# Token weights in blocks of rows, transposed whole, in a new order of steps: a fused attention and MLP kernel on one core

## Chip, cores and metric

One core of one Trainium2 chip. The metric is the device time of one execution in microseconds; lower is better. The core has TensorE (PE; its weight loads are PEld), VectorE (DVE), ScalarE (ACT), GpSimd (POOL) and the queue of SyncE (SP), from which all DMAs of this kernel are issued.

## What is computed

Attention over 8 batches of 8 heads, 576 positions, 64 per head; its output, 8 x 576 x 512, is the input x of the second part. Batch and head are b and h, positions s and t.

```
q_d, k_d, v_d = means of q, k, v over groups of 4 positions          # 144 positions
out_up    = repeat(softmax(q_d k_d^T / 8) v_d, 4)                    # coarse attention
out_local = softmax(q k^T / 8 where |s - t| < 4) v                   # band of 7 positions
x         = out_up + out_local, heads side by side                   # 8 x 576 x 512

theta = x @ w_theta
zr, zi = x * cos(theta), x * sin(theta)
y     = w_tok_r @ zr + w_tok_i @ zi                                  # mixes the 576 positions
u     = x + y
out   = u + max(u @ w_ch, 0)
```

Inputs and output are float32; the kernel computes in bfloat16 with float32 sums.

## The kernel before

**A list of steps.** The work is cut into 1191 small steps, each a word of two letters and an argument, and ORDER (lines 57 to 97) is the one list in which all of them are issued. The two letters name a function in STEPS (line 711), which is called for its next tile in a fixed sequence; the argument is either the engine of a copy (v VectorE, a ScalarE, g GpSimd), one or two banks of PSUM, or a staging slot in base 36. After each step `pin` (line 735) ties every instruction to the one before it on its own engine, so that each engine, and the DMA queue of SP, runs its steps strictly in the order of the list. What orders the engines against one another is data alone: a tile, a bank or a slot that must be ready or free.

**Attention.** For each batch four q and four k loads of two heads each (lq, lk, line 287) go to one of 16 staging slots; cq and ck (line 296) cast them to bfloat16, tp (line 303) transposes nine 128x128 pieces into a pair of banks, ev (line 316) copies the pair out as qT or kT. kd and qd are the means over four positions, on GpSimd in two passes (lines 330, 333, 336) or on VectorE in one (line 322). sd, ed, nd, xn, xd and xc are the coarse attention (scores, exponential, product, division, transpose, copy). The local attention goes in three units of windows a batch: ps (scores, line 482), ex (exponential, line 490), mk (mask, line 501), po (product with v, line 511), nm (division, lines 519 and 520), xt (transpose, line 533), and xa (line 541) adds the coarse part into xT. v comes in ten half windows a batch (lv and lw, line 348; cv casts), save for batch 0, whose v comes in four loads (l1, c1, t1, e1, x1; line 372 casts).

**The second part.** th (line 552) is theta for 128 positions, cs (lines 557 and 558) its cosine and sine, xm (line 591) transposes x, zz (line 616) multiplies both into z; tt, ct, zt and zp or dz are the same for the last 64 positions. mx (line 632) is one mixing product: nine accumulated matmuls of z with the transposed token weights WT (128 x 9 x 576) for 128 features and 288 positions (batch 0 takes its four products for positions 0 to 287 first, the others both halves of a feature group in turn); ua (line 637) adds x. ch (line 662) is u @ w_ch, rl (line 667) the maximum and sum, st (line 671) the store. The last 64 positions of two batches share ht, rt, ss and sr (lines 691, 695, 700). For batches 4 to 7 u is transposed by DMA (du, line 641), for 6 and 7 x as well (dx, line 601), and q and k of batch 7 (dk, line 307).

**The token weights.** lb (line 249) loads nine blocks of 128 rows: 0 to 3 of w_tok_r, 5 to 8 of w_tok_i, and 4 the last 64 rows of both. cb (line 259) casts each into uT, which is free until the first batch is mixed. wp (line 267) makes one row group j of WT: five transposes for 128 source positions, one from each block of w_tok_r (even j) or w_tok_i (odd j); the ninth, for the last 64 positions, takes ten transposes of half width. wc (line 277) copies a row group out, 128 x 576. The sequence of row groups is WPJ (line 42). A row group thus needs five cast blocks.

**Warm matmuls.** wm (line 755) issues matmuls on zeros, whose result nothing reads: the argument's second digit counts those of 512 columns, the third gives one of 64 times so many. Six more are issued with the constants (line 226). An argument of two banks is taken by

```
    def pair(w):
        a, b = sorted(int(x) for x in w)
        return PS[:, a:b + 1:b - a, :]
```

and in ORDER before all two-bank arguments are 01, 23, 45 or 67.

Of the kernel before, what the change touches and what calls it, by code (L numbers as in the profile page):

```python
# [14 lines left out]
P = 128  # L15
B = 8
H = 8
S = 576
# [21 lines left out]
HALF = 64  # L40

WPJ = (0, 2, 4, 6, 1, 3, 5, 7, 8)
# [25 lines left out]
lv9 tp23 nm ts cs cqa th4 lq7 xm5 xt01 th6 evv cs tp23 xa zz cqa tt4 ua tp01 kdg cs ct cqg evv ztv th5 lw evv lw xm7
zz cs tp23 mx6 xm4 kdg zp5 qdg ua eva zz cvv ps01 cqa ps23 lv8 xm7 kdg zz zcv lk4 te ex lw mx6 mx4 ua mx5 sd01 mkv lvb
lw ua ex po67 mkv cva ps23 qdg lca lcc utg ed lce nm mx4 cvg ex lcd lvf ua lk1 po01 lk2 sd67 lw po23 ckg nm cqa nm mx5  # L70
ckg ed tp01 cvg ua lq5 eva tp67 mx4 lq0 cca ua up5 evv cvg ua ccg ccg pv23 mkg ucv vda lk3 qdv ps01 ps67 ex up4 mx5
ccv nd23 ex ua nd01 uca kdg ch5 po67 xn ps23 ckg cka lv9 mx4 xn tp01 lw ex mkg rl nm lk6 cva ckg xd5 sd23 ua cqg xcv
xt67 lv7 eva mx4 lw lv4 lw cvg xa lv8 lw ed xt01 po23 po67 th5 ua ch4 cqa ts cs xa nm nm th0 po23 lqb xt67 rl up1 cs
nm kdg th5 xm0 xa cs xm4 tp23 xm6 tt7 mkg cvg zz th0 lqc ucv zz st up1 cvg up5 ch4 eva ucv ckg ct ucv ch1 zz po23 cs
sd67 lve lva rl mkv te ed cvg pv45 lqd lk1 ztg cqg ch0 rl rl lk2 ch1 qdg nm lq3 vda tp67 nd45 rl cqa xm0 lqf eva lw zz
xn nd23 zp1 utg lw xn tp67 zca lk5 lq9 kdg mx0 up1 ua po45 lv0 eva ckg lk7 ps23 nm lw po67 nm ckg lv4 uca mx0 tp45 lk6
qdg mx1 ua xd0 ps67 ua lv8 ex eva xca ckg sd23 xt45 xa lw mx1 mkg st cvg ua ed mx0 ex mx1 mkv ua th0 po23 ua xt45 ts
cs xa xt67 mx1 xm0 xa th4 xm5 lqb zz ua tt0 kdg xm1 cvv ckg cvv th6 ch7 cqg cka cqg cs ct nm cs lvc cqg lk1 ztv tp23
eva lw th0 rl zz cs cqg zz tp67 evv cvg xm4 zz st zp5 zca ch1 rl cva tp23 mx0 po67 ua eva ps45 lw nm po23 lv2 te ex
lv5 mx1 pv67 lke cqg st mx0 po45 dt vda nm lk7 mkv st lqd po23 ckg ua ua qdg sd67 ch1 qdg nm nm ht0 cka ed rt lv3 up6  # L80
up7 cvg ucv uca nd45 kdg cqg nd23 mx0 xn lw xn ps67 ss ps45 ex ex xd2 mx3 tp67 xcv up2 cva ua uca tp45 lq6 rl evv up0
cqg lw eva ch1 ua lvf xt67 ps23 ucv sd45 xa cva st ex lw lq9 rl lk4 mx0 sd23 ed xt67 ua ckg xa lva qdg lw mkv kdv xt45
mx1 cvg th0 ua st lvb mx6 ua lw ed mkg tp23 ts cs utg lw mx7 cqg xa ua up6 po01 po45 cvg eva uca pv23 tt7 nm vda lq0
nm th6 xm0 zz nd45 ct cs ch1 lv1 xn cva st tp23 nd67 cva xn up0 th4 xm5 th6 zz sr eva xm7 xm5 ps23 lv8 lvc rl uca cs
po01 ch4 zz lw cs nm zz ztg ch7 te ex dz xd6 ch5 cvg rl lw lqe utg rl mkg po01 ps23 st mx4 lw lkd up7 cqg cka st ex
up2 uca nm ch3 rl xt01 kdg st st cvg xcv cva qdg ckg ua xa mkg uca po45 pv67 mx2 nm mx0 ua lk6 sd45 vda lk2 rl lq7
xt67 cqg ua ps23 xa mx1 lv5 ed po45 ua lq3 nm st mkv cqg dt ex dk9 sd23 xt67 ckg ed mx0 mkg du xa nd45 ch1 ckg ua po23
xn po67 th0 ts cs th4 tt5 nm cs nd23 rl dkf nm ct cqg evg dka xm1 xm0 mx6 zz th1 th7 cs dk1 cs xm4 xm5 zz ztv xn ua zz
mx6 zz mx4 po23 ua dz xt01 po67 xd5 ua xcv eva lw evg mx4 nm st mx5 eva du xa mx2 ht3 qdg ua mx4 xt01 ua kdg nm ua utg
ps67 du rt cvv du st ps23 kdg ua te ex ex mx5 mx4 ps67 lvb lv0 lw lw qdv xa lv8 sd23 cva xt01 ua mkv xa mkg mx5 ex st  # L90
lv4 ua po67 ua ed nm sd01 ed po23 mkg cvg ch4 ch5 mx0 nm tt1 lw lw cvg cvg rl sr po67 rl dxd po23 ua nm po45 nm ts ct
nm th0 pv67 th1 dx vda ch2 ztg nd45 st st nd67 du xn du xn cs cs du th3 cs th0 xd1 xt45 xt67 rl xcv cs xt23 xa utg dxc
ch1 dx zz ch0 ch4 xa ss ch5 dz th6 zz ch7 dt du xa tt2 zz th3 dxe dx zz st cs rl th1 mx6 cs mx3 ct st ua rl ztv rl cs
dx7 dx mx2 th6 ht4 rt zz mx1 ua mx0 cs rl mx3 mx6 zz dz rl zz ua ua zz mx7 mx1 mx2 ua ua mx0 ua mx3 ua mx6 ua ua mx1
st ua du mx0 st mx2 ua ss utv ch3 ua ua ua st ua utv ch2 ch1 ch0 ch7 ch6 du ch4 du du du du st rl sr rl du du rl dt
ch1 st st rl st rl st st rl rl ht0 rl st st rm su rt sr ss st
# [4 lines left out]
def kernel(  # L101
# [11 lines left out]
    nc = tc.nc  # L113
# [19 lines left out]
    def bank16(w):  # L133
        return PS[:, int(w), :].bitcast(BF16)
# [20 lines left out]
    rl = tiles(2, [P, 2, 4], "rl", FP32)  # L155
# [6 lines left out]
    cs = tiles(NCS, [P, 2, DM], "cs")  # L162
# [96 lines left out]
    def cb(i, w):  # L259
        to = uT[0][:, i, :] if i < 5 else uT[1][:, i - 5, :]  # L260
        COPY[w](out=to, in_=at.pop(("wtok", i)))

    at = {}

    def wp(j, w):
        ps = at["wp", j] = bank16(w)
        for ri in ((j % 2,) if j < 8 else (0, 1)):
            lo, n = (0, P) if j < 8 else (HALF * ri, HALF)  # L270
            for ct in ((0, 1, 2, 3, 4), (4, 0, 1, 2, 3))[ri]:
                base = P * ct - (HALF if ct == 4 and ri else 0)
                nc.tensor.transpose(out=ps[lo:lo + n, base:base + P],
                                    in_=(uT[ri][:, ct, :] if ct < 4 else uT[0][:, 4, :])[:, P * (j // 2):P * (j // 2) + n],
                                    identity=ident)

    def wc(j, w):
        COPY[w](out=WT[:, j, :], in_=at.pop(("wp", j))[:, 0:S])
# [520 lines left out]
```

## Time and profile before

| | us |
|---|---|
| median of 3 runs | 238.1 (236.89 to 238.81) |
| span of the profiled execution, first to last instruction | 232.1 |
| the runs' median less that span | 6.0 |
| TensorE, VectorE, ScalarE, GpSimd busy in it | 220.7, 191.8, 156.1, 135.5 |
| first mixing product (L632) starts | 37.26 |
| last matmul ends | 227.1 |

The profiled execution's own time around its span is not listed apart. Lines of the profile read: line of the kernel, engine, operation, output <- input, shapes and count; behind them busy microseconds and the mean nanoseconds of one, then how long the engine idled just before and what ended it. In a timeline the two leading numbers are the start and the length in microseconds of the instructions merged in the line. Matmuls follow one another faster than their listed length, which includes their way through the array. A wait names who waited, for what, the total, how often and the longest.

### The profile page before, as it was taken

To read this page: it belongs to the slowest core of one execution; us is meant where nothing else is said; L and a number is where in the kernel's file an instruction comes from. 1 tells how busy PE (TensorE), PEld (TensorE's weight loads), DVE (VectorE), ACT (ScalarE), POOL (GpSimd) and SP (SyncE) were. 2 spreads that over 40 slices of the span, in tenths; PEclk is the share of its full clock that TensorE was granted. 3 is DMA by queue.
4 is the path that set the end of the run, shared out by engine and by line. 5 is a ranking of instruction groups with operands and counts; after the bars stand their busy time and mean duration, and the time that the engine had idled before them with its cause. 6 is when DMAs were issued, how large, how long until landed. Compare 5 with 4: busy or idle time off the path is not lost.

```text
span 232.1 us, 9462 instructions
## 1 busy us (share of the span) xinstructions
PE 220.7 (95%) x3986; PEld 153.2 (66%) x3986; DVE 191.8 (83%) x365; ACT 156.1 (67%) x241; POOL 135.5 (58%) x179
## 2 busy tenths in 40 slices
PE   7998899999998999999999999999999998999991
PEld 2665678777776765776768766676676563767750
DVE  6699999989997988868997997799889967567572
ACT  3359999799877989867976979857766591620000
POOL 7468989869999656897472837767386510000000
PEclk9999999999999999999999999999999999999998
DMA  6999989999999899989606895899957766556676
GB/s 204 382 392 390 298 134 252 365 263 193 264 263 195 224 290 208 203 209 210 174 3 178 226 234 147 293 249 173 153 122 189 144 138 100 154 126 182 138 235 217
DMA packets 76795, 49.41 MB, mean 213 GB/s; under 512 B 61136, under 2 KB 61392, under 8 KB 76752
## 3 DMA queue, kind: packets, MB, share of 16 engines
q1 hardware_dynamic: 76752, 48.81, 84.6%
q8 instruction: 31, 0.51, 1.1%
q14 instruction: 12, 0.10, 0.2%
HBM read 33.98 MB, written 9.44 MB: 187 GB/s over the span
## 4 chain that ended last, share of the span: by engine, by line
PE 72%; DVE 12%; DMA 5%; SPq 3%; issue 3%; ACT 2%; DVEq 0%
PE PS L632 24%; PE PS L662 10%; PE PS L552 9%; PE PS L303 5%; PE PS L755 4%; PE PS L511 3%; DVE xT L541 3%; DMA out_dram<-osb 2%; DVE pm L501 2%; PE PS L591 2%; PE PS L482 2%; DMA st<-xT 2%; SPq L641 2%; PE PS L533 2%; DVE uT L637 2%
## 5 line engine op out<-in xcount | busy, mean ns | idle before, releaser
L632 PE MATMUL PS<-WT,z 128*128 128x288 bf16 x576 | 77.9, 286 | 1.7 <-issue 1.7
L632 PEld LDWEIGHTS <-z 128*128 128x128 bf16 x576 | 53.8, 98 | 17.5 <-issue 2.8
L637 DVE TENSOR_TENSOR uT<-PS,xT 128x288 bf16<-128x288 f32 x64 | 28.1, 450 | 11.4 <-PE PS L632 11.1
L552 PE MATMUL PS<-wth,xT 128*128 128x512 bf16 x128 | 32.3, 380 | 0.7 <-DVE xT L541 0.7
L557 ACT ACTIVATE cs<-PS,pihc 128x512 bf16<-128x512 f32 x32 | 22.3, 696 | 15.1 <-PE PS L552 9.9
L662 PE MATMUL PS<-wch,uT 128*128 128x512 bf16 (+1 forms) x132 | 30.6, 373 | 0.0
L520 DVE TENSOR_TENSOR tmp<-PS,rl 128x512 bf16<-128x512 f32 x40 | 27.7, 692 | 1.4
L541 DVE TENSOR_TENSOR xT<-PS,xdT 128x928 bf16<-128x928 f32 (+1 forms) x24 | 22.7, 952 | 3.4 <-PE PS L533 3.1
L490 ACT ACTIVATE pm<-PS 128x1024 bf16<-128x1024 f32 (+1 forms) x24 | 20.4, 877 | 7.0 <-PE PS L482 2.7
L501 POOL TENSOR_TENSOR pm<-pm,band 128x1024 bf16<-128x1024 bf16 (+1 forms) x13 | 22.2, 1709 | 2.9 <-ACT pm L490 2.9
L667 DVE SCALAR_TENSOR_TENSOR osb<-PS,ur 128x512 f32<-128x512 f32 (+1 forms) x33 | 21.8, 669 | 2.4 <-PE PS L662 1.6
L330 POOL TENSOR_TENSOR two<-kT 128x580 f32<-128x580 bf16 x15 | 17.5, 1163 | 6.1 <-ACT kT L316 5.2
L296 POOL CAST q_tm<-st 128x576 bf16<-128x576 f32 x22 | 14.4, 664 | 10.8 <-DMA st<-in_q_dram 10.8
L662 PEld LDWEIGHTS <-uT 128*128 128x128 bf16 x132 | 12.2, 98 | 12.2 <-issue 0.3
L558 ACT ACTIVATE cs<-PS 128x512 bf16<-128x512 f32 x32 | 19.4, 605 | 0.0
L330 POOL TENSOR_TENSOR two<-qT 128x576 f32<-128x576 bf16 x11 | 12.8, 1167 | 10.5 <-ACT qT L316 7.1
L552 PEld LDWEIGHTS <-xT 128*128 128x128 bf16 x128 | 11.2, 98 | 10.7 <-issue 1.3
L616 DVE TENSOR_TENSOR z<-PS,cs 128x1024 bf16<-128x1024 bf16 x24 | 16.2, 685 | 1.9 <-PE PS L591 0.9
L437 ACT ACTIVATE pd<-PS 128x864 bf16<-128x864 f32 x16 | 14.1, 889 | 5.2 <-PE PS L426 5.2
L761 ACT ACT_TABLE_LOAD x13 | 16.7, 1283 | 0.2
L296 POOL CAST k_tm<-st 128x576 bf16<-128x576 f32 x21 | 14.4, 695 | 1.4 <-DMA st<-in_k_dram 1.4
L396 POOL CAST v_w<-st 128x512 bf16<-128x512 f32 x21 | 13.3, 653 | 1.3 <-DMA st<-in_v_dram 1.2
(119 smaller groups left out, 419.3 us busy)
## 6 DMA issues: line engine op xcount, KB each, us to landing
st<-in_q_dram SPq DMA_DIRECT2D x32, 288.0 KB, 6.3
st<-in_k_dram SPq DMA_DIRECT2D x32, 288.0 KB, 6.0
st<-in_v_dram SPq DMA_DIRECT2D x70, 128.0 KB, 4.7
out_dram<-osb SPq DMA_DIRECT2D x31, 256.0 KB, 2.9
out_dram<-osb SPq DMA_DIRECT2D x10, 128.0 KB, 2.4
st<-in_v_dram SPq DMA_DIRECT2D x4, 288.0 KB, 3.7
st<-in_moe_w_tok_r_dram SPq DMA_DIRECT2D x4, 288.0 KB, 6.2
st<-in_moe_w_tok_i_dram SPq DMA_DIRECT2D x4, 288.0 KB, 7.2
```

What stands on the lines that cost most here:

```text
L296: COPY[w](out=to[:, r, :], in_=of[:, r, :])
L330: nc.gpsimd.tensor_tensor(out=t, in0=src[:, :, 0:2], in1=src[:, :, 2:4], op=ALU.add)
L490: nc.scalar.activation(out=pm[(3 * b + u) % NPM][:, :, 0:n].rearrange("p e c j w -> p e (c j w)"), in_=at.pop(("ps", b, u))[:, :, 0:4 * W ...
L501: EW[w].tensor_tensor(out=t, in0=t, in1=m, op=ALU.mult)
L520: nc.vector.tensor_tensor(out=tmp[(NCH * b + c) % NTMP].rearrange("p g (j d) -> p g j d", d=D), in0=ps[:, :, :, 0:D], in1=r.unsqueeze(3).t ...
L541: nc.vector.tensor_tensor(out=xT[b % 2][:, :, lo:lo + cnt].rearrange("p e (m j) -> p e m j", j=4), in0=at.pop(("xt", b, u))[:, :, 0:cnt].r ...
L552: nc.tensor.matmul(out=ps, lhsT=xT[b % 2][:, dc, P * c:P * c + P], rhs=wth[:, dc, :], start=(dc == 0), stop=(dc == 3))
L557: nc.scalar.activation(out=t[:, 0, :], in_=ps, func=AF.Sin, bias=pihc, scale=1.0)
L632: nc.tensor.matmul(out=ps, lhsT=z[b % 2][:, j, P * dc:P * dc + P], rhs=WT[:, j, cols], start=(j == 0), stop=(j == 8))
L637: nc.vector.tensor_tensor(out=uT[b % 2][:, dc, cols], in0=at.pop(("mx", b, i)), in1=xT[b % 2][:, dc, cols], op=ALU.add)
L662: nc.tensor.matmul(out=ps[:, cols], lhsT=uT[b % 2][:, dc, P * c:P * c + P], rhs=wch[:, dc, cols], start=(dc == 0), stop=(dc == 3))
L667: nc.vector.scalar_tensor_tensor(out=o[:, cols], in0=at["ch", b, c][:, cols], scalar=0.0, in1=ur[b % 2][:, c, cols], op0=ALU.max, op1=ALU.add)
```

## The change

Three things. First, the sequence of the token-weight blocks, for loads, casts, transposes and copies alike: WTI = (0, 5, 1, 6, 2, 7, 3, 8, 4), real and imaginary rows in turn, in place of 0 to 8 for loads and casts and WPJ for the rest. Second, wp and wc work on one block of rows instead of one row group of WT: block i is transposed in five whole 128x128 pieces, the fifth from its last 128 columns (448 to 575), of which the lower 64 output partitions alone are used; wc copies four pieces at once into the 128 columns of every second row group, and a tail of 64 partitions into row group 8. Block 4 holds the last 64 rows of both weights: its four pieces fill columns 512 to 575 of all eight row groups, and it has two tails of 64 columns.

Third, ORDER is a new list of 1190 words. All steps are there as before; the places, engines, banks and slots are others, and two-bank arguments may be any two neighbours (34, 56 and 12 among them; pv, which takes two single banks, has 47 once and 36 once). Besides the places these counts change: warm matmuls, 40 of 512 columns and 31 times 64 columns before, 24 and 24 after; q and k casts on ScalarE, GpSimd and VectorE, 20, 43 and 1 before, 13, 32 and 19 after; q/k evictions (ev) 21, 2 and 9 before, 24, 2 and 6 after; query means (qd) 11 on GpSimd and 5 on VectorE before, 16 on GpSimd after; masks (mk) 13 on GpSimd and 11 on VectorE before, 16 and 8 after; v casts 11, 21 and 8 on ScalarE, GpSimd and VectorE before, 17, 17 and 6 after.

```diff
-WPJ = (0, 2, 4, 6, 1, 3, 5, 7, 8)
+WTI = (0, 5, 1, 6, 2, 7, 3, 8, 4)
...
-l10 l11 l12 c1v c1a c1g k0 l13 kcv wm061 t101 c1g lq4 e1v wm256 t123 lk5 lk6 kca e1v wm483 x12 x13 lk7 ckv lq8 x10 cka
...
-zz zz lw qdv lk8 wcv eva ct lk4 lq9 cs cbg cbg cbg cbg wp6 wca wp3 wp2 wp4 wp5 wca wp1 wcv wcv wcv wp2 ztg ps67 ps45
-qdg wcv te ex wcv ex lq7 kdg lkb lka zz lkc lqe lkd zp1 zcv cvv lqf mx3 cvg cvg cvg mkv ua cvg lq1 mx2 sd01 ps67 lv0
...
+l10 l11 l12 c1a c1a kcv wm730 t101 e1a l13 c1v c1v lk4 wm755 t101 ckv lk5 ckv kcg e1a wm743 tp67 lk6 cka lq7 lq8 cqg
+kcg x10 x11 x12 x13 eva cqg cvv cva kdg cvv cva lk0 x14 ckv wm540 tp01 tp23 cvv lq1 cqv eva qdg lq9 cqv lk2 lka lk3
+pv47 eva wm617 tp56 eva lb4 cka lq5 vdv wm152 ps67 la6 ex ps01 ex ckv qdg tp45 kdv wm327 sd67 sd23 kcv mkv po01 ckv
+cbg mkg ed po67 nm cqg nm la7 ed nd23 la8 cag nd01 cag caa ps67 eva wp4 la0 cag xn xn ex po23 mkg po56 lb1 lq9 cqa lvb
+lba cbg cba xd7 xca nm tp01 eva ts lb2 xt23 lqc nm xa xt56 xa wp7 lqd lb4 po01 th2 cqg nm wp3 cqg lk3 th5 xt01 wcv wcv
+th6 cbg xa cbg xm7 lbe lv8 lv6 wcv cs qdg ckg xm4 lw cs zz zz tt0 xm1 lb0 lba tp23 wp7 lv9 cs lbc ct eva zz th6 wcv
+lqd lq2 ztv wp0 cbg wp1 xm7 wcv cs zp2 cvg cbg cbg zca cbg tp34 lw lv4 wcv wp6 lq1 wp5 zz eva te wcv wp0 mx7 lk7 ps34
...
+    def wtb(i):
+        return uT[0][:, i, :] if i < 5 else uT[1][:, i - 5, :]
...
-    def wp(j, w):
-        ps = at["wp", j] = bank16(w)
-        for ri in ((j % 2,) if j < 8 else (0, 1)):
-            lo, n = (0, P) if j < 8 else (HALF * ri, HALF)
-            for ct in ((0, 1, 2, 3, 4), (4, 0, 1, 2, 3))[ri]:
-                base = P * ct - (HALF if ct == 4 and ri else 0)
-                nc.tensor.transpose(out=ps[lo:lo + n, base:base + P],
-                                    in_=(uT[ri][:, ct, :] if ct < 4 else uT[0][:, 4, :])[:, P * (j // 2):P * (j // 2) + n],
-                                    identity=ident)
-
-    def wc(j, w):
-        COPY[w](out=WT[:, j, :], in_=at.pop(("wp", j))[:, 0:S])
+    def wp(i, w):
+        ps = at["wp", i] = bank16(w)
+        for c in range(4):
+            nc.tensor.transpose(out=ps[:, P * c:P * c + P], in_=wtb(i)[:, P * c:P * c + P], identity=ident)
+        nc.tensor.transpose(out=ps[:, 512:512 + P], in_=wtb(i)[:, S - P:S], identity=ident)
+
+    def wc(i, w):
+        ps = at.pop(("wp", i))
+        if i == 4:
+            COPY[w](out=WT[:, 0:8, 512:S].rearrange("p (c x) t -> p c x t", x=2),
+                    in_=ps[:, 0:512].rearrange("p (c x t) -> p c x t", x=2, t=HALF))
+            tails = [(ri, 512, HALF * ri, HALF) for ri in range(2)]
+        else:
+            COPY[w](out=WT[:, i // 5:8:2, P * (i % 5):P * (i % 5) + P], in_=ps[:, 0:512].rearrange("p (c t) -> p c t", t=P))
+            tails = [(i // 5, P * (i % 5), 0, P)]
+        for ri, to, of, n in tails:
+            COPY[w](out=WT[HALF * ri:HALF * ri + HALF, 8, to:to + n], in_=ps[HALF:P, 512 + of:512 + of + n])
...
-        wp=(wp, [(j,) for j in WPJ]), wc=(wc, [(j,) for j in WPJ]),
+        wp=(wp, [(j,) for j in WTI]), wc=(wc, [(j,) for j in WTI]),
```

More of the change, by code (lines that the diff above doesn't have):

```diff
@@ L68 @@
[L68 to L72, printed above, removed]
@@ L97 @@
+cs rt cs ch7 ss ct ztg ch6 rl mx0 ua mx7 ua st st zz zz zz mx0 mx7 mx1 dz mx2 ua zz mx0 mx3 mx4 ua mx7 ua ua utv rl ua
+ua ua du mx0 ua ua mx7 mx0 mx6 ua ua ch7 st du ch0 ch1 ch2 ua du du du du du rl ch7 uta sr rl rl st du rl rl st st dt
+st st st ch0 rl st ch2 rl st ch7 rm rl su st ht0 rt ss sr k0
 """
@@ L257, in lb @@
             nc.sync.dma_start(out=t, in_=moe_w_tok_i[P * (i - 5):P * (i - 5) + P, :])
+    at = {}
+    def wtb(i):
+        return uT[0][:, i, :] if i < 5 else uT[1][:, i - 5, :]
     def cb(i, w):
[L260 to L278 removed]
+        COPY[w](out=wtb(i), in_=at.pop(("wtok", i)))
+    def wp(i, w):
[14 more added lines that the diff above has]
+            COPY[w](out=WT[HALF * ri:HALF * ri + HALF, 8, to:to + n], in_=ps[HALF:P, 512 + of:512 + of + n])
     def load(n):
@@ L711 @@
     STEPS = dict(
-        k0=(lambda i, w: None, span(1)), kc=(kc, span(4)), la=(la, span(4)), ca=(ca, span(4)), lb=(lb, span(9)), cb=(cb, span(9)), lc=(lc, span(4)), cc=(cc, span(4)),
-        wp=(wp, [(j,) for j in WPJ]), wc=(wc, [(j,) for j in WPJ]),
+        k0=(lambda i, w: None, span(1)), kc=(kc, span(4)), la=(la, span(4)), ca=(ca, span(4)), lb=(lb, [(i,) for i in WTI]), cb=(cb, [(i,) for i in WTI]), lc=(lc, span(4)), cc=(cc, span(4)),
+        wp=(wp, [(j,) for j in WTI]), wc=(wc, [(j,) for j in WTI]),
         lk=(load(0), span(B, 4)), lq=(load(1), span(B, 4)), ck=(cast(0), span(B, 4)), cq=(cast(1), span(B, 4)),
```

60 lines of the change are left out of this document (29 added, 31 removed).

## The prediction

> **What bounds the kernel now.** I read the page's busy times first, then the busy time by stretches, then the timeline of each engine up to the first mixing product (L632, the token-weight matmul that every batch needs), and last the waits of the load queue.
>
> ```profile
> PE 220.7 (95%) x3986; PEld 153.2 (66%) x3986; DVE 191.8 (83%) x365; ACT 156.1 (67%) x241; POOL 135.5 (58%) x179
> ...
> L755 PE MATMUL PS<-warm 128*128 128x512 bf16 (+5 forms) x48 | 11.6, 380 | 0.0
> ```
> ```profile
> 0.00:18.34 18.34, 17.08 (x148) 9.12 (x149) 14.21 (x38) 8.03 (x13) 11.65 (x33) 1.00 0.92 329
> 18.34:37.26 18.92, 17.18 (x505) 13.38 (x505) 18.38 (x35) 18.86 (x29) 16.75 (x22) 1.00 0.98 259
> 37.26:227.10 189.84, 186.41 (x3337) 130.70 (x3334) 158.56 (x294) 129.19 (x201) 107.11 (x126) 1.00 0.85 198
> 227.10:232.10 5.00, 0.00 (x0) 0.00 (x0) 0.67 (x1) 0.00 (x0) 0.00 (x0) 0.85 0.62 192
> ```
>
> The columns of a stretch are its length, then busy PE, PEld, DVE, ACT, POOL, the granted clock, the DMA share and GB/s. There are two regimes. From 37.26 us, where the first mixing product starts, to the last matmul at 227.1 us TensorE is busy 186.4 of 189.8 us: the end of the kernel is that start plus 189.8 us of matmuls, plus 5.0 us in which the last eviction and store finish. Before it TensorE is padded with warm matmuls (11.6 us over the kernel, all ahead of 37.26), and from 18.3 to 37.3 us it is VectorE (18.38 of 18.92) and ScalarE (18.86) that have no room. So the change is judged by one date, the start of the first mixing product, and by whether the 189.8 us behind it stay as dense.
>
> ```profile
> 18.34 0.87 PE L482 MATMUL PS<-qT,kT 64*64 64x64 bf16 x80
> ...
> 34.12 2.32 PE L273 MATMUL PS<-ident,uT 128*128 128x128 bf16 x40
> 36.38 0.72 PE L482 MATMUL PS<-qT,kT 64*64 64x64 bf16 x64
> ...
> 37.26 2.37 PE L632 MATMUL PS<-WT,z 128*128 128x288 bf16 x18
> ```
> ```profile
> 18.67 1.35 DVE L322 TENSOR_REDUCE qd<-qT 128x288 bf16<-128x1152 bf16 x1
> 19.97 0.69 DVE L501 TENSOR_TENSOR pm<-pm,band 128x1024 bf16<-128x1024 bf16 x1
> ...
> 34.90 2.27 DVE L278 COPY WT<-PS 128x576 bf16<-128x576 bf16 x6
> 37.08 0.68 DVE L616 TENSOR_TENSOR z<-PS,cs 128x1024 bf16<-128x1024 bf16 x1
> ```
>
> The 40 last transposes of the token weights stand together at 34.1 us, their evictions on VectorE from 34.9 to 37.1, then the last product z, and the mixing begins. That block is what the change takes apart.
>
> **The change part by part.** *Transposes (wp).* 45 whole 128x128 transposes take the place of 40 whole and 10 half ones; 40 last 2.3 us, so this saves about 0.3 us, ahead of the mixing. *Evictions (wc).* Nine 128x576 copies (seven on VectorE, two on ScalarE) become nine 128x512 copies with strided output and ten tails of 64 partitions, all on VectorE.
>
> ```profile
> L278 DVE COPY WT<-PS 128x576 bf16<-128x576 bf16 x7 | 2.7, 450 | 0.0
> L278 ACT COPY WT<-PS 128x576 bf16<-128x576 bf16 x2 | 1.3, 733 | 0.0
> L649 DVE COPY ur<-PS 128x512 bf16<-128x512 bf16 x6 | 2.4, 417 | 0.8 <-PE PS L646 0.8
> L519 DVE RECIPROCAL rl<-PS 128x8 f32<-128x8 f32 x40 | 8.0, 199 | 1.1 <-PE PS L511 0.8
> ```
>
> A main copy is the 417 ns row. No row is a 64x128 copy out of PSUM: the lower bound is the reciprocal of 8 elements (199 ns), the upper the 417 ns row; I take 0.2 us, being so few elements. Run behind one another they overlap (six in 2.27 us above, 0.38 each), so a block costs about 0.55 us instead of 0.38. In all VectorE has 5 us for the weights instead of 2.7.
>
> *Which blocks the first product needs.* Columns 0 to 287 of every row group of WT come from blocks 0, 5, 1, 6, 2 and 7, the first six in the new order; in the order of steps the first mixing product stands ahead of the evictions of the last two. *Loads (lb).* The same ten DMAs, begun after 15 other loads instead of 23 and spread over more of the queue: the sixth block is complete at 8.85 MB of the queue, the last needed block of before at 9.60. *Banks.* A pair of neighbouring banks is the same instruction with another address: nothing by itself.
>
> *The order of steps.* Counting the words of both orders: warm matmuls fall from 40 full and 31 of 64 columns to 24 and 24, some 3.6 us less of padding. The q and k casts go from 20 ACT, 43 POOL, 1 DVE to 13, 32, 19; VectorE gives up five query means, three q/k evictions, both v evictions at the start and three masks. By the mean times of the rows VectorE's sum moves by -1 us, ScalarE's by +5 (161), GpSimd's by -2: none comes near TensorE's 206 us without padding.
>
> Now the date, step by step. First scores (ps of batch 0), at 18.34 before:
>
> ```profile
> 4.31 0.67 ACT L372 CAST z<-st 128x576 bf16<-128x576 f32 x1 [2.22 <-DMA st<-in_v_dram]
> ...
> 9.82 0.67 ACT L296 CAST q_tm<-st 128x576 bf16<-128x576 f32 x1
> ...
> 12.30 0.59 ACT L394 CAST v_w<-PS 128x512 bf16<-128x512 f32 x1 [1.04 <-PE PS L389]
> ...
> 16.16 1.12 ACT L316 COPY kT<-PS 128x1152 bf16<-128x1152 bf16 x1 [2.13 <-PE PS L303]
> 17.20 1.12 ACT L316 COPY qT<-PS 128x1152 bf16<-128x1152 bf16 x1
> ```
> ```profile
> 7.08 0.67 POOL L372 CAST z<-st 128x576 bf16<-128x576 f32 x1 [0.18 <-DMA st<-in_v_dram]
> ```
> ```profile
> 7.80 0.68 PE L377 MATMUL PS<-ident,z 128*128 128x128 bf16 x9
> ```
> ```profile
> 8.48 0.33 SPq L287 DMA_DIRECT2D st<-in_q_dram  x1
> 9.23 0.33 SPq L287 DMA_DIRECT2D st<-in_k_dram  x1
> ```
>
> All four q/k evictions of batch 0 and both v evictions are now ScalarE's. The fourth v load lands at 7.08 us; cast 0.6, nine transposes 0.68, a ScalarE eviction of 1.12 and the hand-overs: about 9.7 us. Behind that on ScalarE come one cast (0.6), one eviction (1.04 from start to start), two v casts (0.5 each) and three evictions (1.04, 1.04, 1.12): 15.5 us if nothing is waited for. Loads follow one another every 0.75 us (8.48, 9.23), so the twelfth is there at 13.1, cast by 13.8 and transposed by 14.5, in time for the last eviction at 14.4 to 14.6. With some hand-overs: first scores at 16.0 us, 2.3 us earlier. The first mask on VectorE followed the scores by 1.63 us (18.34 to 19.97); so 17.6 us.
>
> From the first mask to the last z product VectorE worked without a gap, 19.97 to 37.76, 17.8 us. In the new order it drops, between the same two marks, a theta cast (0.4), xc (0.4), a k eviction (1.3), a query mean (1.3) and seven weight evictions (2.7), and has a k cast (0.5), zt (0.4) and six block evictions (6 x 0.55 = 3.3): 1.9 less, 15.9 us. The mixing began 0.18 us after the last z product did, 0.5 us before its end: 17.6 + 15.9 - 0.5 = 33.0. VectorE is now nearer to its producers and will wait; I allow 1.0 us for that (it had 0.5 idle in that stretch before): **34.0 us**.
>
> GpSimd, which casts eight of the nine blocks, must not be later:
>
> ```profile
> 20.86 2.12 POOL L501 TENSOR_TENSOR pm<-pm,band 128x1024 bf16<-128x1024 bf16 x1 [0.94 <-ACT pm L490]
> ...
> 24.11 1.15 POOL L501 TENSOR_TENSOR pm<-pm,band 128x512 bf16<-128x512 bf16 x1
> 25.27 1.15 POOL L330 TENSOR_TENSOR two<-kT 128x580 f32<-128x580 bf16 x1
> 26.50 0.67 POOL L333 TENSOR_TENSOR kd<-two 128x290 bf16<-128x290 f32 x1
> ...
> 29.50 3.86 POOL L261 CAST uT<-st 128x576 bf16<-128x576 f32 x6
> ```
>
> From its first mask (near 18.5) it has two masks (3.3), twelve casts of about 0.63 (q, k, theta and blocks; 7.6) and one mean (1.8) up to the sixth block's cast: near 31 us, while that block's eviction is due near 32.5.
>
> Behind that date: before, five score units stood ahead of the first mixing product, now three, so two (x64, 0.65 us) move behind it; all other matmuls ahead of it are the same in number. End: 34.0 + 189.84 + 0.65 + 5.0 = 229.5 us of span against 232.1. The median of the runs is 238.1, that is 6.0 above the profiled span, taken as what lies around it: **235.5 us**, 2.6 less. The start alone can err from 33.0 to 35.5.
>
> **A wait that moves.** Stores now stand closer behind their additions in the load queue (at least a quarter with no TensorE work between, where before nine in ten had 0.9 us), and behind each stand v and q/k loads, whose casts ScalarE and GpSimd run in order. I counted for every load the TensorE work between the last thing that SP must wait for ahead of it and the cast that takes it: the median falls from 16.3 to 11.5 us.
>
> **The rivals.**
>
> *SP is stopped and the loads are late (slower).* Before, it did happen once:
>
> ```profile
> SPq L700 <- DVE rd L457: 10.9, 1, 10.9
> ```
> ```profile
> POOL q_tm L296 <- DMA st<-in_q_dram: 5.3, 1, 5.3
> ```
> ```profile
> 111.00:122.00 11.00, 11.00 (x195) 7.53 (x194) 10.12 (x21) 9.54 (x15) 6.74 (x8) 1.00 0.27 71
> 122.00:135.00 13.00, 13.00 (x297) 10.02 (x295) 11.61 (x17) 10.24 (x14) 7.71 (x9) 1.00 0.76 201
> ```
> ```profile
> st<-in_q_dram SPq DMA_DIRECT2D x32, 288.0 KB, 6.3
> ```
>
> A tail store held SP for 10.9 us, GpSimd waited 5.3 us for a q load, and TensorE lost nothing: 10.9 plus 6.3 to landing is 17.2, against a lead of 16.3. With a lead of 11.5 the same stop costs 5.7 us: 241.2. It decides from a stop of about 5 us on. Against it: most other SP waits in the trace are under 2 us. Chance 0.17.
>
> *The start is won and given back in the middle (no change).* ScalarE has 4 us more behind the first mixing product, and the scores of the last batch come after 151 us of TensorE work instead of 164, so the same evictions are packed closer. If ScalarE's 4 us show on TensorE whole, 239.5; half, 237.5. For it: ScalarE waited in the old trace mostly for TensorE, so it had slack. Chance 0.14.
>
> *The first mixing product waits for all nine blocks*, because the strided evictions are held to overlap its columns, and the early order does not do what it says: three more block evictions, 1.65 us: 237.2. Chance 0.07.
>
> *The clock.* With 16 fewer warm matmuls TensorE pauses more in the start.
>
> ```profile
> 1.26 2.74 PE L226 MATMUL PS<-warm 128*128 128x512 bf16 x6 [1.26 <-DVE warm L197]
> 3.79 2.26 PE L755 MATMUL PS<-warm 128*128 128x512 bf16 x7
> ...
> 12.19 1.74 PE L755 MATMUL PS<-warm 128*128 128x512 bf16 x8
> ```
>
> The first six come 0.42 us apart (1.26 to 3.79), the eight at 12.2 about 0.2. A second such slow stretch of nine matmuls (3.8 us) would cost half of it, 1.9 us: 237.4. The Trainium skill, TensorE: Matmul & The Clock Gate, section "Part 1: The HAM clock gate", says that an idle window of some 3.4 us sets the array back to half rate, whatever came before; the trace agrees in the two spacings and has no fall back, for up to 18.34 TensorE idled 1.26 us, all of it ahead of its first matmul. My walk through the new start has no pause above 1.1 us, so chance 0.03.
>
> *More is won*: no waiting in the start (33.0) and half of the 3.4 us in which TensorE idled behind it gone too, since an order that may take any two neighbouring banks waits less for banks: 232.8. Chance 0.19.
>
> **How the numbers follow.** Forecast 0.40, the rivals 0.17, 0.14, 0.07, 0.03 and 0.19. One per cent, about what a measurement of this kernel can tell from no change, is 2.4 us: 235.7 and 240.5. The forecast's own range is 234.2 to 237.0; 0.25 of its 0.40 lies below 235.7. Faster: 0.25 + 0.19 + a little of the middle rival, 0.45. Slower: 0.17 and the worst of the middle rival, 0.18. Same: 0.37. Range 232.8 to 240.6.
>
> **What would show it.** Right: first scores near 16 us, first mixing product near 34, transposes L273's successor in nine groups of five between 21 and 34 us, warm matmuls near 8 us busy, TensorE busy above 98% from there on. Wrong: the first mixing product at 36 or later, or TensorE idle behind it above 6 us with a load or a ScalarE eviction named as what ended it; that would point to the rivals in their order.

## The result and the profile after

The changed kernel takes 255.5 us, median of 4 runs (251.9 to 255.9), against 237.5 us (235.0 to 238.8, 4 runs) for the kernel before: a ratio of 1.0735, 95% interval 1.0607 to 1.0863. A ratio is taken over the fast executions alone, those within 1.5% of the fastest of the same kernel, so it can differ from the quotient of the medians. The forecast was 235.5 us with a range up to 240.6. The profiled execution took 255.5 us itself, and its span is 253.8, so what lies around a span is 1.7 us and not the 6.0 that the prediction took; the profile of before (232.1) came from one of that kernel's quicker executions.

All lines from the changed constants on have moved down by 5 (L632 is now L637). First the busy line and the granted clock of the page, then the granted clock of before, then the same four stretches as before, cut at the first scores, the first mixing product and the last matmul.

```profile
PE 225.1 (89%) x3962; PEld 154.9 (61%) x3962; DVE 205.3 (81%) x406; ACT 160.3 (63%) x244; POOL 136.2 (54%) x168
...
PEclk9998699999997999799999999999999999999998
```
```profile
PEclk9999999999999999999999999999999999999998
```
```profile
0.00:17.50 17.50, 14.84 (x132) 8.17 (x133) 12.84 (x44) 10.73 (x13) 10.30 (x30) 1.00 0.92 334
17.50:41.56 24.06, 18.78 (x433) 14.08 (x433) 22.70 (x43) 18.60 (x28) 19.10 (x24) 0.86 1.06 252
41.56:247.60 206.04, 191.13 (x3398) 132.62 (x3397) 168.28 (x318) 130.93 (x205) 106.78 (x114) 0.98 0.78 174
247.60:253.80 6.20, 0.36 (x2) 0.00 (x0) 1.45 (x3) 0.00 (x0) 0.00 (x0) 0.86 0.74 254
```

The first scores come at 17.50 us (18.34 before), but the first mixing product at 41.56 (37.26 before), and the stretch behind it is 206.0 us long instead of 189.8, with TensorE idle for 14.9 us of it instead of 3.4 and busy 4.7 us longer, at a granted clock of 0.98 instead of 1.00. So of the 21.7 us that the span grew, 4.3 are lost ahead of the mixing, 16.2 behind it and 1.2 in the tail. VectorE works 13.5 us more, where the prediction had 1 us less, and the clock digit falls to 8, 6, 7 and 7 in four slices ahead of the last, where before it stood at 9.

Where VectorE's time went stands in the groups that keep shapes apart (busy us, mean ns of one, idle before):

```profile
L301 DVE CAST k_tm<-st 128x512 bf16<-128x512 f32 x11 | 9.2, 838 | 2.2 <-DMA st<-in_v_dram 1.8 <-DMA st<-in_k_dram 0.4
...
L301 DVE CAST k_tm<-st 128x64 bf16<-128x64 f32 x11 | 6.3, 572 | 0.0
...
L301 DVE CAST q_tm<-st 128x512 bf16<-128x512 f32 x8 | 5.7, 714 | 0.0
...
L301 DVE CAST q_tm<-st 128x64 bf16<-128x64 f32 x8 | 5.7, 714 | 0.0
```

On VectorE a q or k cast is two instructions, eight rows and one row. The 19 casts take 26.9 us, 1.42 each, and a q piece of 64 columns takes as long as one of 512. The profile of before had one such cast, 427 and 189 ns, and the prediction took its 0.6 us for all 19. Another row of before, which the prediction did not read, said otherwise for the same shape:

```profile
L396 DVE CAST v_w<-st 128x512 bf16<-128x512 f32 x5 | 4.1, 826 | 0.0
```

What makes a cast long is seen where the clock falls first. The timelines of VectorE, GpSimd and TensorE in the changed kernel around 21 us:

```profile
20.53 0.69 DVE L506 TENSOR_TENSOR pm<-pm,band 128x1024 bf16<-128x1024 bf16 x1
21.14 2.92 DVE L301 CAST k_tm<-st 128x512 bf16<-128x512 f32 x2
```
```profile
20.57 2.63 POOL L506 TENSOR_TENSOR pm<-pm,band 128x1024 bf16<-128x1024 bf16 x1 [0.39 <-DVE band L231]
23.15 0.86 POOL L301 CAST q_tm<-st 128x576 bf16<-128x576 f32 x1
```
```profile
22.51 0.40 PE L457 MATMUL PS<-vd,pd 128*72 128x130 bf16 x4
25.08 0.63 PE L452 MATMUL PS<-vd,pd 128*72 128x65 bf16 x8 [2.16 <-DVE tmp L525]
```

The cast starts at 21.14 behind a mask that GpSimd began at 20.57 and does not get on until that mask ends at 23.2; its two pieces take 2.92 us. The divisions (tmp) stand behind it on VectorE, and TensorE, which wants the bank they read, stands still for 2.16 us. Of the 38 pieces of these casts, the eight that no GpSimd instruction overlapped took 427 ns (eight rows) and 180 to 188 ns (one row); every longer one overlapped one. Behind that pause the granted clock is 0.50 for six microseconds (stretches of 2 us, the clock is the last figure but two):

```profile
22.00:24.00 2.00, 0.67 (x12) 0.56 (x12) 2.00 (x2) 1.71 (x3) 2.00 (x3) 0.85 1.00 336
24.00:26.00 2.00, 0.92 (x12) 0.83 (x11) 1.87 (x6) 0.00 (x0) 1.68 (x4) 0.50 0.91 295
26.00:28.00 2.00, 2.00 (x61) 1.60 (x60) 1.88 (x5) 1.44 (x3) 0.76 (x1) 0.50 0.90 306
28.00:30.00 2.00, 2.00 (x73) 1.80 (x74) 1.33 (x4) 1.60 (x3) 2.00 (x4) 0.50 1.07 212
```

It is the same behind the first mixing product: three casts in a row take 3.82 us, and TensorE stands still behind them for 2.22 us.

```profile
97.17 3.82 DVE L301 CAST q_tm<-st 128x512 bf16<-128x512 f32 x6
```
```profile
101.70 4.44 PE L667 MATMUL PS<-wch,uT 128*128 128x512 bf16 x12 [2.22 <-DVE ur L654]
```

The Trainium skill, SBUF — State Buffer, section "Who interferes with whom", says that a copy or cast of VectorE in a mode with two ports and any instruction of GpSimd exclude each other for a whole instruction, and that VectorE outside these modes, with at most one input in SBUF, is not held. The 2.35 us of the eight-row piece against 427 ns agree with the first half, and the runs below test the second.

The waits (total, times, longest) show two more things that before hardly had: SP waits for the sums that it is to store (1.7 us before, beside the one stop of 10.9 us that the prediction shows), and v casts on ScalarE and GpSimd, which work in order, wait for loads (1.2 us before).

```profile
SPq L676 <- DVE osb L672: 12.5, 7, 7.5
```
```profile
POOL v_w L401 <- DMA st<-in_v_dram: 7.4, 3, 4.8
...
ACT v_w L401 <- DMA st<-in_v_dram: 4.2, 4, 2.3
```

### The profile page after: what moved, and what is told of

Read it like the earlier page. It is cut to its first block, busy times and chain, and to the rows that moved or that the text cites. A ratio compares the mean times of both kernels' runs of the same rounds, so it can differ in the third digit from the quotient of the medians.

```text
span 253.8 us, 9436 instructions
## 1 busy us (share of the span) xinstructions
PE 225.1 (89%) x3962; PEld 154.9 (61%) x3962; DVE 205.3 (81%) x406; ACT 160.3 (63%) x244; POOL 136.2 (54%) x168
## 4 chain that ended last, share of the span: by engine, by line
PE 44%; DVE 18%; DMA 16%; issue 7%; SPq 6%; POOL 5%; ACT 2%; DVEq 0%; POOLq 0%; ACTq 0%
PE PS L637 16%; DMA st<-in_v_dram 7%; PE PS L667 6%; PE PS L557 4%; DMA st<-in_q_dram 4%; DVE q_tm L301 3%; PE PS L308 3%; POOL two L335 3%; DVE k_tm L301 3%; DMA out_dram<-osb 3%; PE PS L516 2%; SPq L353 2%; DVE osb L672 1%; PE PS L760 1%; PE PS L538 1%
## 5 line engine op out<-in xcount | busy, mean ns | idle before, releaser
L637 PE MATMUL PS<-WT,z 128*128 128x288 bf16 x576 | 79.0, 289 | 3.9 <-DVE osb L672 2.0
L637 PEld LDWEIGHTS <-z 128*128 128x128 bf16 x576 | 54.7, 98 | 20.6 <-issue 5.2
L506 POOL TENSOR_TENSOR pm<-pm,band 128x1024 bf16<-128x1024 bf16 (+1 forms) x16 | 28.8, 1803 | 14.5 <-ACT pm L495 14.1
L667 PE MATMUL PS<-wch,uT 128*128 128x512 bf16 (+1 forms) x132 | 32.6, 388 | 2.3 <-DVE ur L654 2.2
L562 ACT ACTIVATE cs<-PS,pihc 128x512 bf16<-128x512 f32 x32 | 22.1, 692 | 14.8 <-PE PS L557 13.4
L335 POOL TENSOR_TENSOR two<-qT 128x576 f32<-128x576 bf16 x16 | 18.7, 1169 | 9.9 <-DVE qT L321 6.2
L335 POOL TENSOR_TENSOR two<-kT 128x580 f32<-128x580 bf16 x14 | 16.5, 1181 | 9.6 <-ACT kT L321 9.1
L578 POOL TENSOR_TENSOR zT<-xT,cst 128x512 bf16<-128x512 bf16 x4 | 4.6, 1152 | 26.8 <-ACT cst L575 26.8
L321 ACT COPY kT<-PS 128x1152 bf16<-128x1152 bf16 x12 | 13.4, 1120 | 6.9 <-PE PS L308 6.1
L301 DVE CAST k_tm<-st 128x512 bf16<-128x512 f32 (+1 forms) x22 | 14.6, 705 | 2.2 <-DMA st<-in_v_dram 1.8
```

The lines of the kernel that those rows point to most:

```text
L301: COPY[w](out=to[:, r, :], in_=of[:, r, :])
L335: nc.gpsimd.tensor_tensor(out=t, in0=src[:, :, 0:2], in1=src[:, :, 2:4], op=ALU.add)
L506: EW[w].tensor_tensor(out=t, in0=t, in1=m, op=ALU.mult)
L562: nc.scalar.activation(out=t[:, 0, :], in_=ps, func=AF.Sin, bias=pihc, scale=1.0)
L637: nc.tensor.matmul(out=ps, lhsT=z[b % 2][:, j, P * dc:P * dc + P], rhs=WT[:, j, cols], start=(j == 0), stop=(j == 8))
L667: nc.tensor.matmul(out=ps[:, cols], lhsT=uT[b % 2][:, dc, P * c:P * c + P], rhs=wch[:, dc, cols], start=(dc == 0), stop=(dc == 3))
```

## The experiments

Four theories: A, the casts on VectorE are held by GpSimd; B, loads are late in the new order; B2, stores are late in it; C, the new order is slow on TensorE itself, by its banks and its in-order engines, whatever the others do. Medians in us; a ratio is to the kernel before in the same series.

**The weights alone** (the new wp, wc and WTI with the ORDER of before):

> The new transposes, copies and sequence of the token weights in the order of steps of before, so that only the first part of the change is in. Theory A: within 1% of before, 236 to 240 us, for it has no more casts on VectorE than before; VectorE's weight copies take some 2 us more ahead of the first mixing product, which may come 1 us later. Rival D (the weights' evictions are what costs): 245 us or more.

237.2 us, ratio 1.0078 (1.0023 to 1.0132). The whole transposes and the eviction by blocks are not the loss: they cost about a per cent, and the first mixing product comes at 39.5 us with them instead of 37.26. The rest of the loss is in the new list.

**The 19 casts on ScalarE:**

```diff
+            w = "a" if w == "v" else w
```

> The changed kernel with its 19 q/k casts of VectorE moved to ScalarE, all else as it is. Theory A (a VectorE cast out of SBUF stands still while a GpSimd instruction runs, so these casts cost 1.4 us each instead of 0.6): VectorE busy falls from 205 to about 178 us, ScalarE rises from 160 to 173, the first mixing product comes at 38 us or earlier and the time falls to 240 us, 237 to 244. Rival B (late loads behind closer stores in the load queue): the loads stay as they are, 253 us or more. Rival C (the new order leaves TensorE waiting for banks and evictions, whatever casts): no change, 252 us or more.

252.3 us, ratio 1.0702 (1.0572 to 1.0833). VectorE's sum falls from 205.3 to 183.2 us, and the time by only 3. Theory A had 237 to 244 us, so as the whole cause it fails here.

**The same 19 casts on VectorE in the kernel before**, in two pieces and then in one piece of nine rows:

```diff
+            w = "v" if (n, b, hh) in ONV else w
...
-            for r in ((slice(0, WR - 1), slice(WR - 1, WR)) if w == "v" else (slice(0, WR),)):
+            for r in (slice(0, WR),):
```

> The kernel before with the same 19 casts (those of the same batch and head pair) put on VectorE, all else as it is. Theory A: each costs VectorE about 1.2 to 1.4 us and delays what stands behind it: VectorE busy 191.8 to about 215 us, the time 245 to 255 us. Rivals B and C: the order and the load queue are those of before, 236 to 240 us.

> The kernel before with the same 19 casts of q and k put on VectorE as in the earlier run (247.0 us), but in one piece of nine rows. Theory A (the price is that of casts held by GpSimd, and nine rows in one piece, 737 to 753 ns in every case, are not held): 19 x (1.1 - 0.74) = 7 us of VectorE come back of the 15 that the two-piece casts cost, and the time falls to 239 to 243 us. If the cost were the engine's share of work alone, whatever the form, it stays at 246 to 248 us.

247.0 us, ratio 1.0507 (1.0369 to 1.0645), and 243.9 us, ratio 1.0368 (1.0273 to 1.0462). The groups of the two kernels, two pieces first:

```profile
L299 DVE CAST k_tm<-st 128x512 bf16<-128x512 f32 x11 | 6.0, 541 | 0.1
...
L299 DVE CAST q_tm<-st 128x512 bf16<-128x512 f32 x8 | 5.0, 625 | 1.2 <-DMA st<-in_q_dram 1.2
...
L299 DVE CAST k_tm<-st 128x64 bf16<-128x64 f32 x11 | 3.9, 358 | 0.0
...
L299 DVE CAST q_tm<-st 128x64 bf16<-128x64 f32 x8 | 2.6, 331 | 0.0
```
```profile
L299 DVE CAST k_tm<-st 128x576 bf16<-128x576 f32 x11 | 8.1, 743 | 0.1
...
L299 DVE CAST q_tm<-st 128x576 bf16<-128x576 f32 x8 | 5.9, 741 | 0.0
```

Casts on VectorE cost the old order 9.5 us by the medians and some 12 by the ratio. The change of form brings 3.2 of that back (17.5 us of casts become 14.0); I had expected 4 to 8, from 1.1 us a cast in two pieces, and this trace has 0.92. The other 6 to 9 us stay with the casts on VectorE in either form, and most of them are lost ahead of the first mixing product, which comes at 44.3 and 42.1 us instead of 37.26. So the part of theory A that speaks of form explains only the smaller share.

**One piece of nine rows in the changed kernel** (the last edit alone):

> The changed kernel with each VectorE q/k cast as one instruction of nine rows (576 elements) instead of eight rows and one. Theory A: halves the number of times that VectorE can be held; if nine rows go one element a cycle and leave GpSimd alone, a cast takes 0.66 us beside GpSimd or not, and the time falls to 240 to 245 us; if it is held like the others, about 0.9 us a cast and 247 to 252 us. Rivals B and C: no change, 252 us or more.

251.3 us, ratio 1.0682 (1.0547 to 1.0816). Its casts, with minimum, median and maximum in ns:

```profile
L301 DVE CAST k_tm<-st x11: 742/744/753, 7.8 to 155.9; 128x576 bf16<-128x576 f32 x11
L301 DVE CAST q_tm<-st x8: 737/742/744, 12.9 to 145.7; 128x576 bf16<-128x576 f32 x8
```

All nineteen lie between 737 and 753 ns, where the pieces of eight rows had lain between 414 and 2349: the slower form is never held. The second half of that rule of the Trainium skill (its section "Who interferes with whom") has it so if this form is outside the modes with two ports; the trace shows its time and not its mode. The first scores come at 16.3 us and the first mixing product at 38.1. The time itself moved by little more than the spread: four executions of the changed kernel took 251.9 to 255.9 us, four of this one 249.6 to 253.2. 14 us of the loss stay.

**Loads left out**, in three kernels: the changed one, the one before, and the changed one with one-piece casts.

```diff
+            if b:
+                at["s", n, b, hh] = cin9
+                return
...
-        at["v", b, c] = stg[int(w, 36)][:, 0:DM]
-        half_v(b, c, 0)
+        at["v", b, c] = cin8
```

> The changed kernel, casts of q and k as they are (two pieces on VectorE), but the loads of q, k and v of the batches 1 to 7 left out: the casts read 64 constants over and over instead, so the output is not the reference's. Every cast, transpose and product stays. Theory B (loads come late in the new order, and ScalarE and GpSimd, which work in order, stand in front of them): the waits of v casts for v loads (11.6 us on the two engines in the changed kernel) go, and what they pull behind them; what stays is the price of the held casts, 5 to 9 us over the kernel before: 242 to 247 us. Theory C (the order itself is slow on TensorE, banks and engines in order, whatever the loads do): 251 to 256 us. Theory A (held casts alone): 251 to 256 us too.

> The kernel before with the same loads left out (the output is not the reference's), as the yardstick of the run beside it. Its trace shows almost no engine waiting for a load behind the first 30 us, so theories A, B and C all expect 233 to 237 us, at most 2% under the kernel before. If it falls far more, loads cost both kernels, and only the difference of the two counts.

> The changed kernel with both suspects out: casts of q and k on VectorE in one piece of nine rows (747 ns, mostly not held; 251.3 us with loads), and the loads of the batches 1 to 7 left out (the output is not the reference's). Theory B: 237 to 241 us, at most 4 us above the kernel before without loads. Theory C: 247 to 252 us, since neither casts nor loads were the cause of the 14 us that the one-piece casts left.

247.8 us (ratio 1.0497, 1.0403 to 1.0591), 232.1 us (0.9833, 0.9743 to 0.9923) and 240.2 us (1.0179, 1.0076 to 1.0282). The first two lie just outside what was expected, 247.8 above theory B's 242 to 247 and 232.1 below 233. The loads cost every kernel something: 4.9 us the one before, 7.7 and 11.1 the two with the new order. So B holds in part, but 8.1 us were left between the last two figures, more than the 4 that it allowed.

**Stores moved up**, since the trace with one-piece casts shows this stall behind 217 us. SP, VectorE, TensorE:

```profile
209.82 1.20 SPq L691 DMA_TRANSPOSE utr<-ut  x1
211.07 2.56 SPq L606 DMA_TRANSPOSE st<-xT  x2
213.67 1.06 SPq L676 DMA_DIRECT2D out_dram<-osb  x2
```
```profile
218.94 0.69 DVE L700 SCALAR_TENSOR_TENSOR osb<-PS,utr 128x512 f32<-128x512 f32 x1 [3.38 <-DMA out_dram<-osb]
219.55 0.68 DVE L672 SCALAR_TENSOR_TENSOR osb<-PS,ur 128x512 f32<-128x512 f32 x1
```
```profile
220.28 2.00 PE L637 MATMUL PS<-WT,z 128*128 128x288 bf16 x15 [2.39 <-DVE osb L672]
```

Two stores whose sums were ready at 209 us stand on SP behind three transposes by DMA and are issued at 213.7. Until the second has landed, VectorE cannot write the next osb tile; it waits 3.38 us, the evictions wait behind it, and TensorE waits 2.39 us for a bank. The edit moves them, and one store of batch 0, ahead of the transposes and loads:

```diff
-rl st utv th1 th2 th7 zz ch6 ch3 cs utv ht1 dt dx rl dxe st st dx
+rl st st st utv th1 th2 th7 zz ch6 ch3 cs utv ht1 dt dx rl dxe dx
```

> The changed kernel with one-piece casts (251.3 us), and three stores moved up in SP's order: the stores of (4,2) and (4,3) from behind the turning of ut(2) and two transposes of xT to right behind the store of (4,1), and the store of (0,0) from behind five loads to ahead of them. The trace with one-piece casts shows TensorE idle for 2.4 us at 217.9, behind an eviction that stands on VectorE behind an osb tile whose store was issued at 214.2 and landed 4.5 us later. Theory B2 (part of what is left is SP's order: stores late, tiles late, VectorE in order): that stall goes, 2 to 3.5 us less, 248 to 249.5 us. Theory C (banks and engines): no change, 251 us, the stall comes back under another name.

> The changed kernel with one-piece casts, without the loads of the batches 1 to 7 (the output is not the reference's; 240.2 us), and with the same three stores moved up. Theory B2: 237 to 238.5 us, so that 5 to 6 us over the kernel before without loads (232.1) are left for the order itself. Theory C: 240 us.

247.4 us (246.3 to 249.2; ratio 1.0544, 1.0415 to 1.0673) against 251.3 (249.6 to 253.2), and without loads 237.2 us (236.3 to 238.0; ratio 1.0053, 1.0015 to 1.0091) against 240.2 (238.9 to 241.4). TensorE's wait of 2.4 us for that bank is gone from both traces. Theory B2 holds: 3 to 4 us were three words of the list.

The second of these still stood 5.1 us over the kernel before without loads, which looked like theory C. But its VectorE timeline has a held cast again:

```profile
19.34 2.41 DVE L320 CAST k_tm<-cin 128x576 bf16<-128x576 f32 x1
```

There the casts of the later batches read 64 constants nine times over; such a cast takes 481 ns free and can be held. So the run without loads had brought theory A back by its stand-in. With a whole staging slot as the stand-in:

```diff
-    cin = one([P, D], "cin", FP32)
+    cin = stg[11]
```

> The run before (one-piece casts, stores moved up, loads of the batches 1 to 7 left out, 237.2 us) once more, with one thing mended: there the casts of the batches 1 to 7 read 64 constants nine times over, and its trace shows that VectorE casts of that kind take 481 ns when free and up to 2407 ns behind GpSimd; here they read a whole staging slot of constants that no load uses, as the one-piece casts with loads do (737 to 753 ns). The output is not the reference's. If the 5.1 us over the kernel before without loads (232.1) that were left there are this hold come back (it starts with a cast of 2.41 us at 19.3 that leaves TensorE idle for 1.75 us, and a granted clock of 0.66 behind it): 232 to 235 us, so that held casts, late loads and late stores are the whole of the loss. Theory C (banks and engines in the new order): 236 to 238 us.

```profile
L320 DVE CAST k_tm<-st x11: 742/744/755, 7.1 to 142.6; 128x576 bf16<-128x576 f32 x11
L320 DVE CAST q_tm<-st x8: 735/742/744, 12.7 to 132.5; 128x576 bf16<-128x576 f32 x8
```

234.0 us (232.7 to 234.8), ratio 0.9963 (0.9914 to 1.0012). That is 1.9 us over the kernel before without loads. That kernel still reads the 64 constants, but it has no cast of the later batches' q and k on VectorE, and its five v casts there take 855 ns as against 826 with loads, so it hardly shares the effect. Theory C is left with about these 1.9 us.

**Half of v not loaded** asks why the loads are late: the queue is full, or slots and SP's order hold them up.

```diff
     def lw(b, c, w):
-        half_v(b, c, 1)
+        pass
```

> The changed kernel with one-piece casts and stores moved up (247.4 us), and the second half of every load of v of the batches 1 to 7 left out: the casts still stand where they stood and read the whole slot, so the output is not the reference's. That takes 35 of 70 issues of 0.6 us and 4.6 of 28.9 MB of input off the one queue, and changes neither order nor slots. In the trace v casts waited 19.2 us for loads of v, while the queue was full from 10 to 110 us. If what the queue can deliver is the limit (the new order asks for more of it ahead of the same mixing products), these waits fall under 6 us and the time to 236 to 241 us. If the loads are late because slots come free late or SP stands behind other things, the time stays at 244 to 247 us.

237.1 us (235.7 to 238.2), ratio 1.0023 (0.9983 to 1.0062), from 247.4. The waits for v with all of v loaded,

```profile
POOL v_w L412 <- DMA st<-in_v_dram: 12.8, 7, 4.2
...
ACT v_w L412 <- DMA st<-in_v_dram: 9.1, 5, 3.8
...
DVE v_w L412 <- DMA st<-in_v_dram: 2.1, 1, 2.1
```

24.0 us together, are all gone in the other. The run takes out bytes and SP's issues together, so it does not tell a queue short of bytes from one short of issues; the DMA engines' share below speaks for bytes. Two stretches each of the kernel before, of the changed one with its two mends, and of that with half of v; the share of the DMA engines is the last figure but one:

```profile
20.00:60.00 40.00, 38.21 (x905) 29.68 (x904) 37.97 (x71) 37.59 (x59) 34.41 (x43) 1.00 1.02 259
60.00:100.00 40.00, 38.30 (x800) 27.58 (x802) 33.95 (x67) 32.67 (x50) 32.62 (x40) 1.00 1.05 239
```
```profile
20.00:60.00 40.00, 34.16 (x743) 25.76 (x747) 32.90 (x71) 28.75 (x43) 31.10 (x41) 0.91 1.09 252
60.00:100.00 40.00, 34.73 (x678) 24.65 (x681) 33.06 (x59) 31.44 (x51) 33.10 (x37) 0.96 1.02 229
```
```profile
20.00:60.00 40.00, 33.62 (x770) 25.54 (x774) 35.83 (x75) 31.45 (x48) 34.74 (x45) 1.00 0.97 262
60.00:100.00 40.00, 38.38 (x827) 28.07 (x830) 36.17 (x70) 34.33 (x56) 34.99 (x40) 1.00 0.89 232
```

In the old order too the queue is full from 20 to 100 us, and it moves the same 230 to 260 GB/s; there it is hidden, with TensorE busy 76.5 of 80 us. The new order gets the same supply and wants more of it sooner. Counting words: ahead of the ninth mixing product stand 29 casts of q and k and 11 of v in the old list, 32 and 12 in the new; ahead of the 25th, 49 and 25 against 52 and 31. At 288 KB a cast of q or k and 256 KB one of v that is 1.1 and 2.4 MB more, at some 250 GB/s an estimated 4 and 10 us of a full queue. The runs without loads show it in time too: by 60 us the new order has run 31 casts of q and k and 7 of v, the old 29 and 5; by 100 us 48 and 19 against 43 and 15, 2.5 MB more. Measured, taking the loads out is worth 13.4 us in the new order (247.4 to 234.0) and 4.9 in the old, 8.5 more.

**The account.** From 255.5 us: casts in a form that is not held, -4.2; three stores moved up, -3.9; the loads beyond what they cost the old order, -8.5; left over against the kernel before without loads, 1.9. That makes 18.5, and the kernels differ by 18.0; it closes by the way it is built, and the 0.5 is the kernel before, 237.5 us in one series and 237.0 in another. The terms are differences of medians from series on several chips, where the kernel before had medians of 236.7 to 237.5; the first term lies near the spread of its runs. The terms also depend on their order, since a late load hides a held cast: with the loads in, one-piece casts and moved stores together bring 8.1 us (255.5 to 247.4), with the loads out 13.8 (247.8 to 234.0). No version with all its work in it beat the kernel before.

## Why the prediction was wrong, point by point

**"VectorE's sum moves by -1 us"** failed first. The term is the 18 more casts at 0.6 us. The row that it rests on was one cast of a whole kernel, made while GpSimd was idle; the measured mean is 1.42 us, so that 18 casts come to 14.8 us above their price of 10.8, and the sum moved by +13.5. No rival held that price, although the row of v casts on VectorE in the same profile, 826 ns for the shape that a wth cast did in 420, said that it is not fixed. zt, priced at 0.4, took 1.42 us at 37.97 beside a GpSimd instruction that began at 37.96.

**First scores at 16.0** was right as a chain and wrong as a date: 17.50 with the held casts, 16.3 to 17.0 in the three versions with one-piece casts and all loads or all but half of v, 15.99 in the last run without loads.

**First mixing product at 34.0** failed: 41.56. Without held q and k casts it is 38.1 to 38.5, without later loads too 36.86; so by these single traces some 3 us are held casts with the clock behind them, 1.2 to 1.7 the loads, and 2.9 are left for the walk itself, in which VectorE was to wait 1.0 us, and for the clock, granted at 0.92 in that stretch of the last run too. The parts that concern the weights were nearly right. A block's main copy and tail took 0.42 and 0.23 us, and blocks in a row came 0.66 to 0.70 us apart where 0.55 was the price; VectorE's copies for the weights took 5.9 us in all instead of 5. Three block evictions end behind the start of the first mixing product, so the rival that it waits for all nine falls.

**"End = that start plus 189.84"** failed most: 206.0, with the idle time of TensorE at 14.9 us instead of 3.4. The prediction took the density of the old stretch as a property of the work. It was a property of the old list, in which a full queue and a few late stores happened to have cover.

**The rivals.** Late loads had 0.17 and 241.2 us. Loads came late, but hardly by a single stop of SP. Such a stop did come: SP stood for 7.5 us at 121 us behind a store, GpSimd waited 4.8 us for a v load at 141, and yet TensorE was idle for only 1.0 us from 120 to 150. The loads were late by a queue that was already full, which the quoted stretches showed (DMA share 0.98 and 259 GB/s ahead of the mixing). Worked from that, the rival might have had a larger price. The middle rival put the loss on ScalarE, which TensorE's waits name for 0.5 us. The clock had 0.03 and happened: TensorE's pauses were up to 2.2 us and not the 1.1 of the walk. Its price, 1.9 us, was too low as well: TensorE was busy 4.7 us longer behind the first mixing product, of which the prediction moved 0.65 there, so an estimated 4 us go to the lower clock.

**The range** took the rivals one at a time. Late loads (8.5 us beyond the old order's, against a price of 5.7) and the clock came together, and with them held casts and late stores, which no rival held.

## What to carry to other kernels

Before work is moved to an engine, price it by all rows of that shape on that engine, not by the one cheap row, and ask what the engine beside it is doing at that time; where the means of one shape differ by two, the cheap form may be held by something, and a slower form that is never held can be the better one. A dense stretch belongs to the order that made it: count for a new order how many bytes it wants ahead of each product, and where the queue is full already, more bytes sooner is time lost. A stand-in for work that is left out must keep the form of the instructions that read it, or it brings in an effect of its own.

## What the runs showed of the hardware beyond that

*The clock falls after pauses of 1 to 2 us, and the length of one pause does not decide it.* In the changed kernel TensorE idled for 2.16 us up to 25.08, with shorter pauses ahead of it, and the granted clock was 0.50 from 24 to 30 us; in the run with 64 repeated constants and the stores moved up the longest pause of that stretch was 1.75 us, in the last run without loads 1.00 us, and the clock still fell to 0.50. Yet it stayed at 1.00 behind a pause of 1.92 us at 53.5 in the changed kernel and behind one of 2.19 us at 36.0 in the run with half of v. The Trainium skill, TensorE: Matmul & The Clock Gate, section "Part 1: The HAM clock gate", speaks of an idle window of some 3.4 us; here the measurement decides: none of these pauses was that long. What tells those that cost the clock from those that did not, no run here settles.

*Loads of short rows move more slowly and cost more to issue.* In the profile of before, the DMA engines' share in tenths and GB/s in forty slices of 5.8 us, then SP's issues with minimum, median and maximum in ns:

```profile
DMA  6999989999999899989606895899957766556676
GB/s 204 382 392 390 298 134 252 365 263 193 264 263 195 224 290 208 203 209 210 174 3 178 226 234 147 293 249 173 153 122 189 144 138 100 154 126 182 138 235 217
```
```profile
L348 SPq DMA_DIRECT2D st<-in_v_dram x70: 596/626/2923, 26.3 to 178.0; - x70
L287 SPq DMA_DIRECT2D st<-in_q_dram x32: 327/408/2326, 2.7 to 149.9; - x32
```

The three slices from 5.8 to 23 us, with loads of q, k and weights in rows of 512 floats or more, move 382 to 392 GB/s; those from 29 to 110 us, with loads of v among them in rows of 64 floats, mostly 190 to 290, with the engines nearly full in both. A v load of 128 KB takes SP 626 ns in the median, a q load of 288 KB 408. This fits with half of v being worth 10 us; no run changes the rows alone.
